# Odd units' half-precision casts on VectorE through all 192 units, in place of ScalarE from unit 37 on

## The chip, the cores and the metric

The kernel runs on one core of a Trainium2 chip. Its metric is the device time of one launch in microseconds (us), the median of several runs. The engines have their own in-order instruction streams and wait for each other through semaphores: PE (TensorE, matrix products; PEld is its weight load), DVE (VectorE), ACT (ScalarE), POOL (GpSimd) and SP (SyncE, which here issues the DMAs).

## The reference

Cluster attention is followed by a two-layer MLP. Each query and each key is assigned to the nearest of 16 centroids of its head; a query sees only keys of its own cluster.

```python
mask = q_assign[:, :, :, None] == k_assign[:, :, None, :]
scores = scale * np.matmul(q, k.transpose(0, 1, 3, 2))
scores = np.where(mask, scores, -1000000000.0)
scores = scores - np.max(scores, axis=-1, keepdims=True)
attn = np.exp(scores)
attn = attn / (np.sum(attn, axis=-1, keepdims=True) + 1e-09)
out = np.matmul(attn, v)              # 4 batches, 8 heads, 768 positions, 64 wide
# heads side by side: x is 3072 tokens by 512
h = x @ w_in                          # 512 to 2048
r = np.maximum(h, 0.0)
g = s * (r * r) + b
return g @ w_out                      # 2048 to 512
```

## The kernel before

Attention is cut into 192 units: one head and 128 queries against all 768 keys, in the order batch, chunk of 256 queries, pair of heads, row block, head. The MLP is cut into 192 steps: one chunk of 256 tokens and one block of 128 hidden columns. One loop with the counter i runs both: pass i issues unit i's scores and, 21 passes later (`LAG`), the MLP step that has become possible. So each pass after the beginning holds about one unit and one MLP step.

Single-precision accuracy comes from pairs of half-precision numbers: a value is cast to a high half, and the difference from the cast is the low half. For a unit this is done so:

- `scores`: PE makes the 128x768 scores in one of two PSUM buffers (`sc`, four products, L465).
- `maxima` and `exps`: DVE reduces the row maximum (L474); ACT makes the bias from it (L481) and then the exponentials `p` in single precision (L484). The score buffer is free after that, so PE can make the scores of unit i+2.
- `high`: the cast of `p` to half precision, the upper half of `ph` (L494, through the helper `copy`, whose ACT form has the line L120 and whose DVE and POOL forms have L122). This is the line of the change.
- `low`: POOL subtracts the cast from `p` for the lower half of `ph` (L516), and SP issues a DMA that transposes `ph` into `PT` (L518).
- `values`: PE multiplies `PT` with the two halves of v into the bank `px` (18 products a unit, L535 to L537), and DVE divides by the row sums (L543, L544, L547). `finish_x` splits the result into halves (ACT L558, POOL L561) and transposes it for the MLP (SP L564).

An MLP step is twelve products for `h` (L593) in a single PSUM bank, on ACT a relu that empties the bank (L600) and two squares (L602, L603), a subtraction on POOL for the low half `g` (L608), and six products into `acc` (L620). Beside this, one after the other, run the preparations of the next chunk's queries and the next batch's keys and values (`prep_q`, `prep_k`, `prep_v`): small chains that go through DVE (L102, L99, L69, L371, L188), PE (L98, L396), ACT (L186), POOL (L383, L293) and DMAs (`QA`, `QB`, `KA`, `KB`). The bank named `m` is shared by `px` and by these checks.

The first 16 units take another way (no cast, transposes on PE). Units 16 to 18 are cast on POOL. From unit 19, before the change, odd units up to 35 are cast on DVE, everything else on ACT; unit 37 is where the splitting of the weights, one block a pass for 16 passes, has ended. The order of instructions on each engine isn't that of the program's text: a scheduler places them with its own estimates of time, and so a change of engine in one place moves instructions on all engines.

Of the kernel before, what the change touches and what calls it, by code (L numbers as in the profile page):

```python
# [26 lines left out]
def tile_cluster_attention_mlp(ctx, tc, q, k, v, cent, w_in, w_out, s_in, b_in, out):  # L27
# [10 lines left out]
    NF = DFF // P  # L38
    HALF = S // 2
    V = nc.vector  # L40
    G = nc.gpsimd
    A = nc.scalar
    LAG = 21
# [74 lines left out]
    def copy(eng, dst, src):  # L118
        if eng is A:
            A.activation(dst, src, AF.Copy)  # L120
        else:
            eng.tensor_copy(dst, src)  # L122
# [366 lines left out]
    def high(i):  # L489
        u = U[i]  # L490
        if i < TURN:
            return
        u["ph"] = sb.tile([P, 2, S], F16, tag="big", name=f"ph_{i}", bufs=BIGN)
        copy(G if i < LAG - 2 else V if i < LAG + NF and i % 2 else A, u["ph"][:, 0, :], u["p"])  # L494

    def low(i):
        u = U[i]
# [220 lines left out]
    i = 0  # L718
    while i < NU + 8 or i - LAG < NS + 4:
# [10 lines left out]
        if 0 <= i - 1 < NU:  # L730
            with first_of_all(i):
                high(i - 1)
# [48 lines left out]
```

## Time and profile before

| | us |
|---|---|
| Median of 3 runs | 948.9 (946.03 to 953.5) |
| The profiled execution, its own time | 955.32 |
| Its span, first to last instruction | 953.6 |
| PE busy | 838.4 (88%) |
| ACT busy | 717.1 (75%) |
| DVE busy | 617.1 (65%) |
| POOL busy | 545.1 (57%) |

The profile has four parts in time. To about 140 us the first keys, queries and weights are prepared and PE waits often. From there to about 235 us the weights are split beside the first MLP steps. From 235 us (unit 37) to 882 us (the last cast) each pass holds a unit and an MLP step; this stretch is 647 us long. After 882 us the last MLP steps are left. A row of the profile gives line, engine, operation, tile written and tiles read, shapes, count, busy time, mean duration in ns and the idle time of the engine just before, with what ended it.

### The profile page before, as it was taken

The numbers are of one execution on the slowest core, as the hardware profiler recorded it, in microseconds if no ns is written. First come the engines' busy times: TensorE is split into PE (matmuls) and PEld (weight loads), VectorE is DVE, ScalarE is ACT, GpSimd is POOL, SyncE is SP. The second block draws the span as 40 slices with busy tenths as digits, with TensorE's granted clock in tenths as the row PEclk, the third lists the DMA queues.
The fourth block names the chain that finished last, engine by engine and source line by source line (L and its number), as shares of the span: only waits on it lengthen the run. The fifth ranks groups of instructions, "written<-read, shape, count | busy, mean of one in ns | idle before, by whom it ended". The sixth has DMA issues, their size and how long they took to land.

```text
span 953.6 us, 22551 instructions
## 1 busy us (share of the span) xinstructions
PE 838.4 (88%) x8673; PEld 587.2 (62%) x8673; DVE 617.1 (65%) x1416; ACT 717.1 (75%) x1406; POOL 545.1 (57%) x580
## 2 busy tenths in 40 slices
PE   0568565888999999999998999999999999999997
PEld 0456443565566666767666667666666767677664
DVE  7697888898577656657658667667766466463100
ACT  3476866877678878888777988977887888889443
POOL 3010115666566765777676767757867766676321
PEclk9966575999999999999999999999999999999999
DMA  6888813867777997887786898869779858786100
GB/s 171 217 220 242 238 34 77 200 143 123 178 134 144 200 192 136 167 175 144 144 171 139 196 187 162 165 139 200 131 156 181 149 119 158 137 161 141 33 23 23
DMA packets 437756, 144.23 MB, mean 151 GB/s; under 512 B 405392, under 2 KB 434064, under 8 KB 437648
## 3 DMA queue, kind: packets, MB, share of 16 engines
q1 hardware_dynamic: 437648, 142.78, 70.8%
q8 instruction: 68, 1.11, 0.5%
q14 instruction: 40, 0.33, 0.1%
HBM read 35.69 MB, written 6.29 MB: 44 GB/s over the span
## 4 chain that ended last, share of the span: by engine, by line
PE 31%; DVE 5%; DMA 5%; ACT 5%; POOL 4%; issue 4%; SPq 0%; POOLq 0%; DVEq 0%; ACTq 0%
PE h L593 12%; PE acc L620 11%; PE sc L465 4%; DMA qn<-in_q_dram 2%; POOL g L608 1%; POOL ph L516 1%; DMA kn<-in_k_dram 1%; PE px L535 1%; ACT p L484 1%; PE px L537 1%; PE px L536 1%; DVE ssm L474 1%; ACT ph L120 1%; DMA PT<-ph 1%; ACT r L600 1%
## 5 line engine op out<-in xcount | busy, mean ns | idle before, releaser
L516 POOL TENSOR_TENSOR ph<-p,ph 128x768 f16<-128x768 f32 x176 | 297.7, 1692 | 117.8 <-ACT ph L120 77.5
L620 PE MATMUL acc<-wos,g 128*128 128x512 f16 x1152 | 295.1, 380 | 3.6 <-POOL g L608 3.4
L593 PE MATMUL h<-x,wis 128*128 128x256 f16 x2304 | 288.1, 274 | 7.9 <-ACT r L600 3.7
L593 PEld LDWEIGHTS <-wis 128*128 128x128 f16 x2304 | 222.7, 98 | 59.4 <-issue 12.4
L474 DVE TENSOR_REDUCE ssm<-sc 128x1 f32<-128x768 f32 x192 | 181.8, 950 | 33.9 <-PE sc L465 33.3
L608 POOL TENSOR_TENSOR g<-r,g 128x256 f16<-128x256 f32 x192 | 133.3, 695 | 105.4 <-ACT r L603 103.0
L484 ACT ACTIVATE p<-sc,ssm,qsm 128x768 f32<-128x768 f32 x192 | 187.7, 978 | 1.5
L620 PEld LDWEIGHTS <-g 128*128 128x128 f16 x1152 | 104.4, 98 | 87.7 <-POOL g L608 7.2
L120 ACT ACTIVATE ph<-p 128x768 f16<-128x768 f32 x164 | 136.0, 830 | 5.2 <-DMA PT<-ph 2.9
L481 ACT ACTIVATE ssm<-ssm,lift,qsm 128x1 f32<-128x1 f32 x192 | 73.1, 381 | 87.1 <-DVE ssm L474 86.3
L600 ACT ACTIVATE r<-h,cf 128x256 f32<-128x256 f32 x192 | 89.2, 464 | 62.6 <-PE h L593 53.7
L535 PE MATMUL px<-vh,PT 128*128 128x65 f16 x1104 | 121.1, 196 | 9.0 <-DVE xs L547 2.4
L536 PE MATMUL px<-vl,PT 128*128 128x64 f16 x1104 | 121.0, 193 | 0.0
L537 PE MATMUL px<-vh,PT 128*128 128x65 f16 x1104 | 120.4, 195 | 0.7 <-DVE PT L514 0.7
L465 PE MATMUL sc<-KA,QA 128*128 128x384 f16 x384 | 100.1, 344 | 18.3 <-ACT p L484 15.4
L535 PEld LDWEIGHTS <-PT 128*128 128x128 f16 x1104 | 103.8, 98 | 19.3 <-issue 5.9
L536 PEld LDWEIGHTS <-PT 128*128 128x128 f16 x1104 | 103.6, 100 | 13.5 <-issue 4.8
L465 PE MATMUL sc<-KB,QB 128*128 128x384 f16 x384 | 100.6, 346 | 7.3 <-DMA QB<-qb 7.3
L537 PEld LDWEIGHTS <-PT 128*128 128x128 f16 x1104 | 103.7, 98 | 4.0 <-DVE PT L514 0.8
L602 ACT ACTIVATE g<-r 128x256 f16<-128x256 f32 x192 | 79.3, 413 | 4.3 <-PE acc L620 0.3
L603 ACT ACTIVATE r<-r 128x256 f32<-128x256 f32 x192 | 78.9, 411 | 3.5
L465 PEld LDWEIGHTS <-QA 128*128 128x128 f16 x384 | 36.0, 101 | 46.0 <-issue 20.4
(158 smaller groups left out, 1033.8 us busy)
## 6 DMA issues: line engine op xcount, KB each, us to landing
wst<-in_moe_w_in_dram SPq DMA_DIRECT2D x16, 512.0 KB, 4.5
wst<-in_moe_w_out_dram SPq DMA_DIRECT2D x16, 512.0 KB, 4.5
kn<-in_k_dram SPq DMA_DIRECT2D x16, 384.0 KB, 4.2
qn<-in_q_dram SPq DMA_DIRECT2D x24, 256.0 KB, 3.5
vn<-in_v_dram SPq DMA_DIRECT2D x16, 384.0 KB, 4.1
out_dram<-o SPq DMA_DIRECT2D x12, 512.0 KB, 3.5
PT<-ph SPq DMA_TRANSPOSE x176, 3.5
x<-xn SPq DMA_TRANSPOSE x48, 2.6
```

Of the source, the lines that this page charges most:

```text
L120: A.activation(dst, src, AF.Copy)
L465: last_score[0] = nc.tensor.matmul(sc[:, e, :HALF], X[:, col, :], y[:, h * S + e * HALF : h * S + (e + 1) * HALF], start=st, stop=not st)
L474: last_max[0] = V.tensor_reduce(SM[i // 4][:, 0, j : j + 1], U[i]["sc"], axis=AX.XY, op=ALU.max, negate=True)
L484: last_exp[0] = A.activation(p.rearrange("p (a b) -> p a b", a=2), u["sc"], AF.Exp, bias=bi, scale=u["scale"], **total)
L516: G.tensor_tensor(u["ph"][:, 1, :], u["p"], u["ph"][:, 0, :], op=ALU.subtract)
L535: nc.tensor.matmul(o1, PT[:, kt, :], vh[:, h, kt, : D + 1], start=(kt == 0), stop=False)
L536: nc.tensor.matmul(o, PT[:, kt, :], vl[:, h, kt, :], start=False, stop=False)
L537: nc.tensor.matmul(o1, PT[:, T + kt, :], vh[:, h, kt, : D + 1], start=False, stop=(kt == T - 1))
L593: nc.tensor.matmul(ph[:, :CW], WSP[ft][0][:, wl, kt, :], XS[(b, c, kt)][:, :, xl, :], start=(i == 0), stop=(i == len(terms) - 1))
L600: A.activation(r, ph[:, :CW], AF.Relu, scale=MS[(b, c)][0])
L608: G.tensor_tensor(g[:, 1, :], r, g[:, 0, :], op=ALU.subtract)
L620: nc.tensor.matmul(acc[:, t, :], g[:, gl, rows], WSP[ft][1][:, wl, :], start=(ft == 0 and gl + wl == 0), stop=(ft == NF - 1 and gl == 1))
```

## The change

Casts of odd units from 37 to 191 move from ACT to DVE. Even units stay on ACT. Nothing else is edited.

```diff
     def high(i):
         u = U[i]
         if i < TURN:
             return
         u["ph"] = sb.tile([P, 2, S], F16, tag="big", name=f"ph_{i}", bufs=BIGN)
-        copy(G if i < LAG - 2 else V if i < LAG + NF and i % 2 else A, u["ph"][:, 0, :], u["p"])
+        copy(G if i < LAG - 2 else V if i % 2 else A, u["ph"][:, 0, :], u["p"])
```

The scheduler moves other instructions too: 78 casts leave ACT and come to DVE, and from unit 37 on all five engines have rows in another order. Two places show it.

ACT at units 116 to 118, before. `p_117` is the exponential of unit 117, `ph_117` its cast, `r` and `g` are the MLP's relu and squares.

```order
L120 ACTIVATE ph_116_8871<-p_116_8805 128x768
L484 ACTIVATE p_117_8875<-sc_117_8860,ssm_116_8802,qsm_2_1_0_7950 128x768
L600 ACTIVATE r_2_0_0_8898<-h_2_0_0_8885,cf_2_0_8881 128x256
L602 ACTIVATE g_2_0_0_8900<-r_2_0_0_8898 128x256
L481 ACTIVATE ssm_116_8802<-ssm_116_8802,lift_132,qsm_2_1_0_7950 128x1
L603 ACTIVATE r_2_0_0_8898<-r_2_0_0_8898 128x256
L120 ACTIVATE ph_117_8999<-p_117_8875 128x768
L484 ACTIVATE p_118_9003<-sc_118_8984,ssm_116_8802,qsm_2_1_0_7950 128x768
```

The same place on ACT after the change.

```order
L120 ACTIVATE ph_116_8871<-p_116_8805 128x768
L484 ACTIVATE p_117_8875<-sc_117_8860,ssm_116_8802,qsm_2_1_0_7950 128x768
L481 ACTIVATE ssm_116_8802<-ssm_116_8802,lift_132,qsm_2_1_0_7950 128x1
L600 ACTIVATE r_2_0_0_8898<-h_2_0_0_8885,cf_2_0_8881 128x256
L602 ACTIVATE g_2_0_0_8900<-r_2_0_0_8898 128x256
L484 ACTIVATE p_118_9003<-sc_118_8984,ssm_116_8802,qsm_2_1_0_7950 128x768
```

The cast of the odd unit 117 no longer stands ahead of the exponential of unit 118; one of the squares has moved behind it as well.

DVE at units 175 and 176, before. The rows L543 to L547 are the division of a finished pair of units, `amb_q` a maximum in the preparation of queries.

```order
L474 TENSOR_REDUCE ssm_172_12886<-sc_175_13064 128x1
L543 TENSOR_SCALAR ssm_168_12622<-px_168_12977 128x2
L544 RECIPROCAL ssm_168_12622<-ssm_168_12622 128x2
L547 TENSOR_TENSOR xs_42_13016<-px_168_12977,ssm_168_12622 128x128
L102 TENSOR_REDUCE amb_q3_2_1_13144<-qn_3_2_1_13062 128x2
L543 TENSOR_SCALAR ssm_168_12622<-px_170_13103 128x2
L544 RECIPROCAL ssm_168_12622<-ssm_168_12622 128x2
L474 TENSOR_REDUCE ssm_176_13162<-sc_176_13149 128x1
```

The same place on DVE after the change.

```order
L474 TENSOR_REDUCE ssm_172_12886<-sc_175_13064 128x1
L102 TENSOR_REDUCE amb_q3_2_1_13144<-qn_3_2_1_13062 128x2
L122 CAST ph_175_13160<-p_175_13079 128x768
L543 TENSOR_SCALAR ssm_168_12622<-px_170_13103 128x2
L544 RECIPROCAL ssm_168_12622<-ssm_168_12622 128x2
L547 TENSOR_TENSOR xs_42_13016<-px_170_13103,ssm_168_12622 128x128
L474 TENSOR_REDUCE ssm_176_13162<-sc_176_13149 128x1
```

The cast of unit 175 stands between the maxima of units 175 and 176, ahead of a division that frees the shared bank. Of the 78 new casts 22 stand so, ahead of the next unit's maximum; 39 stand behind the maximum of unit i+1 and ahead of that of i+2, and 17 behind that one as well.

## The prediction

> **What bounds the kernel now.** First the page's busy times and clock, then busy times by stretch: before the change's first unit (35 us of it), the stretch in which it acts, and the end.
>
> ```profile
> PE 838.4 (88%) x8673; PEld 587.2 (62%) x8673; DVE 617.1 (65%) x1416; ACT 717.1 (75%) x1406; POOL 545.1 (57%) x580
> PEclk9966575999999999999999999999999999999999
> ...
> 200.00:235.00 35.00, 30.21 (x347) 20.80 (x348) 31.54 (x64) 27.17 (x56) 24.53 (x23) 1.00 0.70 140
> 235.00:882.00 647.00, 618.64 (x6815) 433.97 (x6813) 412.79 (x939) 524.96 (x1020) 448.01 (x447) 0.99 0.80 159
> 890.00:953.00 63.00, 57.89 (x434) 38.73 (x431) 6.15 (x20) 28.05 (x65) 15.39 (x23) 0.99 0.06 20
> ```
>
> The columns of the last three rows are stretch, length, then busy time of PE, PEld, DVE, ACT and POOL, clock, DMA share and GB/s. Units 37 to 191 lie in the middle row. There PE is busy 618.6 of 647.0 us (96%) at a clock of 0.99, so PE sets the pace and every other engine counts only as far as it makes PE wait. PE is without work for 28.4 us; that is about all that a better distribution can win by this view. ACT is next at 81%, then POOL at 69% and DVE at 64%. The last row has no cast in it: there the change can do nothing.
>
> Next, who made PE wait in the stretch (total us, times, longest):
>
> ```profile
> PE sc L465 <- ACT p L484: 4.3, 7, 1.1
> PE h L593 <- ACT r L600: 3.4, 6, 1.3
> PE pq L396 <- DMA QA<-qa: 3.3, 4, 1.1
> PE am_q L98 <- DVE ksm L99: 3.1, 2, 1.9
> PE h L593 <- DMA x<-xn: 2.7, 3, 1.4
> PE sc L465 <- DMA QB<-qb: 1.9, 2, 1.5
> PE px L535 <- DVE qsm L99: 1.8, 2, 1.5
> PE am_q L98 <- DVE xs L547: 1.7, 2, 1.4
> PE acc L620 <- POOL g L608: 1.6, 3, 0.7
> PE px L535 <- DVE xs L547: 1.4, 1, 1.4
> PE am_q L98 <- DVE amb_q L102: 0.8, 1, 0.8
> PE px L535 <- DVE oe_k L288: 0.7, 1, 0.7
> PE am_q L98 <- DVE vm L99: 0.4, 1, 0.4
> PE pq L396 <- DVE xs L547: 0.3, 1, 0.3
> ```
>
> By releaser: ACT 4.3 + 3.4 = 7.7 us; DVE 3.1 + 1.8 + 1.7 + 1.4 + 0.8 + 0.7 + 0.4 + 0.3 = 10.2 us; DMAs 3.3 + 2.7 + 1.9 = 7.9 us; POOL 1.6 us. ACT is the busier engine, but PE waits more for DVE, mostly in the short checks that share one PSUM bank.
>
> **The change part by part.** What the casts cost on each engine, and what else runs there in the stretch (from the groups by line, and from the rows of the tile `ph`, which give min/median/max in ns):
>
> ```profile
> L516 POOL TENSOR_TENSOR ph<-p,ph x176: 1632/1644/2356, 138.2 to 881.7; 128x768 f16<-128x768 f32 x176
> L120 ACT ACTIVATE ph<-p x164: 825/827/845, 161.9 to 880.8; 128x768 f16<-128x768 f32 x164
> L122 DVE CAST ph<-p x9: 531/551/1017, 159.8 to 235.6; 128x768 f16<-128x768 f32 x9
> ...
> L122 DVE CAST ph<-p 128x768 f16<-128x768 f32 x9 | 5.8, 647 | 0.0
> L120 ACT ACTIVATE ph<-p 128x768 f16<-128x768 f32 x164 | 136.0, 830 | 5.2 <-DMA PT<-ph 2.9 <-DMA KA<-ka 2.0
> L474 DVE TENSOR_REDUCE ssm<-sc 128x1 f32<-128x768 f32 x155 | 146.8, 950 | 26.6 <-PE sc L465 26.0
> ```
>
> *What leaves ACT.* The odd numbers from 37 to 191 are 78, and 78 x 0.830 = 64.7 us leave ACT: 525.0 falls to 460.3, 81% to 71%. In the order before, each of these casts stands directly ahead of the next exponential, as at unit 118, so that exponential can come up to 0.83 us sooner and its score buffer is free sooner. A wait behind a queue grows with its busy time over its free time; I scale with that ratio as an estimate. For ACT it is 525.0/122.0 = 4.3 before and 460.3/186.7 = 2.5 after, a factor 0.57, and 0.43 x 7.7 = **3.3 us less**. The ends are nothing (some of these waits start earlier, at a maximum on DVE) and all 7.7.
>
> *What comes to DVE.* The same cast exists there nine times, at 0.647 us in the mean: 78 x 0.647 = 50.5 us, so DVE goes from 412.8 to 463.3 (72%). The nine come from a time when POOL was no busier (24.5 of 35 us, 70%, against 69%), but one took 1.017 where the least is 0.531, so the price depends on POOL, as these rows of single instructions, and the two groups on DVE that also read two tiles in SBUF, show:
>
> ```profile
> 567.94 1.49 DVE L371 TENSOR_TENSOR qsm<-qsm,ksm 128x2 f32<-128x2 f32 x1
> 567.74 1.67 POOL L516 TENSOR_TENSOR ph<-p,ph 128x768 f16<-128x768 f32 x1 [0.79 <-ACT ph L120]
> L371 DVE TENSOR_TENSOR qsm<-qsm,ksm x24: 141/161/1493, 15.9 to 833.1; 128x2 f32<-128x2 f32 x24
> ...
> L188 DVE SCALAR_TENSOR_TENSOR ka<-kn,ksm,ka x10: 1007/1606/2394, 265.3 to 701.3; 128x768 f16<-128x768 f32 x10
> ...
> L188 DVE SCALAR_TENSOR_TENSOR ka<-kn,ksm,ka 128x768 f16<-128x768 f32 x10 | 16.3, 1628 | 4.1 <-ACT ka L186 4.1
> ```
>
> An operation on two numbers a lane took 1.49 us instead of 0.16 and ended when POOL's subtraction did; the subtraction beside it, which had begun first, took its normal time. The larger `ka` operation loses 1628 - 1007 = 621 ns in the mean. If casts fared as badly they would take 0.531 + 0.621 = 1.152 us, 89.9 us in all. I take the 0.647, the row of the cast itself.
>
> The Trainium skill (SBUF — State Buffer, section "Who interferes with whom") speaks against the change here: a VectorE copy or cast in a two-port mode and a GpSimd instruction shut each other out of a shared port pair, and the one that comes second waits for the whole instruction of the first. The trace agrees for L371 (1.49 us against 0.16); by this rule a cast that comes just after the start of a subtraction would take some 0.55 + 1.64 = 2.2 us (an estimate with the trace's durations), which no cast of this trace shows.
>
> How much of this reaches PE? The cast also adds a wait: DVE has to hold at it until ACT has made `p`. Behind it in DVE's queue stand the next maximum (for which ACT's bias L481 and then the exponential wait) and the division that frees the bank (for which PE waits). For 56 of the 78 the next maximum behind the cast is of unit i+2 or later, whose scores need the buffer that this same exponential frees; there the cast runs while PE refills the buffer and its cover is 0.65 us of PE work. For 22, as at unit 175, it is not so. With the ratio as for ACT: 412.8/234.2 = 1.76 becomes 463.3/183.7 = 2.52, a factor 1.43, and 0.43 x 10.2 = **4.4 us more**. The ends are nothing (all covered) and, at 89.9 us, 502.7/144.3 = 3.48, a factor 1.98, 10.0 us.
>
> *What POOL and the DMAs do.* POOL's subtraction of an odd unit, with its transpose on SP's queue, can start 0.83 - 0.55 = 0.28 us sooner; `PT` is read four passes later, so this wins nothing. Against it, a cast on DVE shuts POOL out as in the rows above, in the other direction (L516's longest is 2.356 against 1.644). If casts meet POOL as often as it is busy (69%), it loses 0.69 x 78 x 0.531 = 28.6 us: 448.0/199.0 = 2.25 becomes 476.6/170.4 = 2.80, a factor 1.24. POOL's own wait and the three DMAs that end chains through it make 1.6 + 7.9 = 9.5 us, and 0.24 x 9.5 = **2.3 us more**; the ends are 2 us less (their ACT links, L186 and L558, come sooner) and, were every cast to meet POOL (78 x 0.531 = 41.4 us), 3.6 us more.
>
> *The rest.* The clock of PE is full and stays so: nothing, within 3 us either way (the mean of 0.99 leaves 0.01 x 647 = 6 us, of which I let half come or go). The first 235 us and the MLP's end keep their instructions: nothing.
>
> The sum is -3.3 + 4.4 + 2.3 = +3.4 us. The profiled execution took 955.3 us, its span of 953.6 and 1.7 around it, and would take 958.7. It is 6.4 us above the median of 948.9, and the difference carries over to the median: 948.9 + 3.4, so **952 us**. The ends of the terms give -7.7 + 0 - 2 - 3 = -12.7 and 0 + 10.0 + 3.6 + 3 = +16.6, that is 936 to 966.
>
> **The rivals.** *ACT was what counted (faster).* If all waits for ACT go (7.7) and with them those for work that starts from ACT, the subtraction `g` (1.6, after L603) and `x` (2.7, after L558), while DVE's 234 us of free time swallows the casts, the time is 948.9 - 12.0 = 936.9. For it speak these waits of the other engines in the stretch:
>
> ```profile
> POOL ph L516 <- ACT ph L120: 77.5, 66, 2.8
> ACT ssm L481 <- DVE ssm L474: 69.2, 67, 3.4
> POOL g L608 <- ACT r L603: 50.5, 47, 2.9
> ```
>
> POOL waits for ACT 128 us in these rows. Against it speaks the middle one: ACT itself waits 69.2 us for DVE's maxima, so what leaves ACT is partly bought with a later maximum.
>
> *DVE's queue is held at the cast (slower).* The place is the 22 casts that stand ahead of the next unit's maximum. There the maximum waits for the exponential and for the cast. If POOL runs as it does beside `ka`, each costs 1.15 us, 22 x 1.15 = 25.3, and with 3.3 back from ACT the time is 948.9 + 22.0 = 970.9; at the casts' own 0.647 it is 14.2 - 3.3, 959.8. The middle is 965. It decides where PE has less than a cast's length to spare at that point. The rule of the skill named above is this rival's reason for the longer casts. Against it: only 26.0 us of DVE's idle time in the row of L474 ends with PE, so DVE often has the scores waiting and isn't on the path each time.
>
> *The new order (either way, rather slower).* The scheduler has moved rows on every engine. If half of some 28 preparations in the stretch (18 of queries, 10 of keys by the group counts) gain a wait like those for `QA` (3.3/4 = 0.8 us), that is 14 x 0.8 = 11.2 us: 960.
>
> ```profile
> L383 POOL COPY qa<-qb 128x512 f16<-128x512 f16 x18 | 13.7, 760 | 0.0
> L333 POOL COPY kb<-ka 128x768 f16<-128x768 f16 x10 | 8.3, 834 | 12.7 <-ACT ka L186 12.4
> ```
>
> That the change does not do what it says is excluded by the order: 78 more casts on DVE, as many less on ACT.
>
> **How the numbers follow.** 1% is 9.5 us (939.4 to 958.4), about what a measurement can tell from no change. My sum has a chance of 0.55: 0.45 within 1%, and 0.10 above by its upper end. ACT's relief has 0.17, counted as faster. The held queue has 0.20, counted as slower. The new order has 0.08: 0.05 slower, 0.03 within. So faster 0.17, same 0.48, slower 0.35. The range is 936 (the lower end, which nearly holds the first rival) to 970 (which nearly holds the second).
>
> **What would show it.** Right: in the stretch ACT near 460 us busy and DVE near 463; a DVE cast of 0.6 to 0.7 us in the mean; PE's waits for `p` and `r` down by some 3 us and those for `ksm`, `qsm` and `xs` up by more. Wrong: casts of 1 us or more with L474's rows later (held queue); PE's waits for DVE unchanged and the stretch over 9 us shorter (ACT's relief); DVE's waits unchanged but `QA`, `QB` or `x` waits doubled (order). A change in the first 235 us or after the last cast would make the whole working wrong.

## The result, and the profile after

The changed kernel takes 964.75 us (median of 4 runs, 961.98 to 968.27) against 951.2 us for the kernel before (4 runs, 946.03 to 956.42): a ratio of 1.012, 95% interval 1.0082 to 1.0157 (the two medians alone would give 1.014; ratios are given as recorded, with their intervals). It is slower by a little more than the 1% that the prediction set as the bound of what can be told.

The profiled execution took 965.98 us, its span is 964.3. First the busy times of the page and the groups that the change touches; the columns are as before.

```profile
PE 836.0 (87%) x8673; PEld 585.6 (61%) x8673; DVE 662.3 (69%) x1494; ACT 667.6 (69%) x1328; POOL 547.5 (57%) x580
...
L120 ACT ACTIVATE ph<-p 128x768 f16<-128x768 f32 x86 | 71.4, 830 | 3.7 <-POOL ph L516 3.2
L122 DVE CAST ph<-p 128x768 f16<-128x768 f32 x87 | 55.7, 640 | 14.9 <-ACT p L484 6.3
```

The change does what it says: 78 casts fewer on ACT, 78 more on DVE, and a cast on DVE takes 640 ns in the mean, where 647 was taken for the sum. DVE and ACT are now equally busy, at 69%. ACT's casts fell by 64.6 us (136.0 to 71.4), but its busy time by only 49.5 (717.1 to 667.6): neighbouring rows on ACT overlap, as where an exponential starts at 342.80, takes 0.99 us and the next row starts at 343.69, and busy time counts an overlap once. PE has no less work than before and needs longer for it.

Where the time went shows when the two executions are cut at the same two places, the start of the exponential of unit 37 and the end of the last exponential. Before:

```profile
0.00:239.00 239.00, 157.64 (x1380) 111.37 (x1381) 200.08 (x461) 162.35 (x317) 81.10 (x110) 0.81 0.68 167
239.00:880.60 641.60, 613.47 (x6774) 430.68 (x6774) 409.82 (x933) 521.53 (x1014) 444.40 (x442) 0.99 0.80 159
880.60:953.60 73.00, 67.29 (x522) 45.16 (x519) 7.19 (x24) 33.27 (x77) 19.59 (x28) 0.99 0.11 30
```

After:

```profile
0.00:241.00 241.00, 153.75 (x1380) 109.23 (x1381) 200.83 (x462) 162.57 (x317) 81.29 (x110) 0.84 0.67 165
241.00:896.10 655.10, 619.85 (x6790) 434.09 (x6790) 453.01 (x1009) 474.58 (x942) 447.05 (x444) 0.99 0.77 156
896.10:964.20 68.10, 62.44 (x505) 42.26 (x502) 8.45 (x25) 30.42 (x71) 19.15 (x27) 0.98 0.13 32
```

The stretch grew by 13.5 us and the end shrank by 4.9, because PE did more of the MLP within the stretch (6.4 us more busy time there, 4.9 less in the end). What is left is 13.5 - 4.9 = 8.6 us. Of it 7.1 us are idle time of PE (33.8 us in stretch and end before, 40.9 after) and 1.5 us a longer busy time for the same products. Another 2.0 us lie ahead of unit 37 (241.0 against 239.0). They are not the change's: in the two traces the rows of every engine are the same up to 242 us, so this is a difference between two executions of the same rows, and not the change in the first part that the prediction had named as a sign against it. The waits of PE in the stretch say where its idle time went:

```profile
PE acc L620 <- POOL g L608: 5.8, 8, 1.4
PE h L593 <- ACT r L600: 5.0, 8, 1.3
PE pk L346 <- DVE xs L547: 3.9, 2, 2.3
PE pq L396 <- DMA QA<-qa: 3.3, 2, 1.7
PE sc L465 <- ACT p L484: 3.2, 4, 1.7
PE am_q L98 <- DVE xs L547: 2.4, 2, 1.7
PE h L593 <- DMA x<-xn: 2.3, 3, 1.5
PE sc L465 <- DMA QB<-qb: 2.2, 1, 2.2
PE px L535 <- DVE xs L547: 1.6, 2, 1.4
PE px L535 <- DVE cf L582: 1.3, 1, 1.3
PE px L535 <- DVE xm L584: 1.0, 1, 1.0
PE px L535 <- DVE xm L99: 0.9, 1, 0.9
PE pq L396 <- DVE xs L547: 0.8, 2, 0.6
PE am_q L98 <- DVE amb_q L102: 0.6, 1, 0.6
PE px L535 <- DVE qsm L65: 0.6, 1, 0.6
PE px L535 <- DVE qsm L99: 0.3, 1, 0.3
```

| PE waits in the stretch for | before | after |
|---|---|---|
| ACT | 7.7 | 8.2 |
| DVE | 10.2 | 13.4 |
| DMAs | 7.9 | 7.8 |
| POOL | 1.6 | 5.8 |
| sum | 27.4 | 35.2 |

The sum rose by 7.8 us, about the 7.1 of idle time. ACT gave nothing back although its busy time in the stretch is 47 us less. Of what came on top, 4.2 us are POOL's, all at `g`, and 3.2 DVE's. This is one execution of each kernel, and runs of the kernel before alone spread from 946.03 to 956.42 us, so a difference of a few us in one row is a sign and no proof. How it comes about can be read at one place. The rows are those of DVE, POOL and PE near 347 us, around the cast of unit 59, whose `p` was ready at 343.79.

```profile
346.45 0.95 DVE L102 TENSOR_REDUCE vm<-vn 128x1 f32<-128x768 f32 x1 [3.24 <-DMA vn<-in_v_dram]
347.32 0.55 DVE L122 CAST ph<-p 128x768 f16<-128x768 f32 x1
...
347.95 1.64 POOL L516 TENSOR_TENSOR ph<-p,ph 128x768 f16<-128x768 f32 x1 [4.11 <-DVE ssm L543]
349.55 0.67 POOL L608 TENSOR_TENSOR g<-r,g 128x256 f16<-128x256 f32 x1
...
350.28 0.39 PE L620 MATMUL acc<-wos,g 128*128 128x512 f16 x1 [1.24 <-POOL g L608]
```

DVE stood 3.24 us at a step of the preparation of v whose load had not landed; the cast stood behind it, though its input was there. POOL, in order too, stood 4.11 us at that unit's subtraction (the profile names L543, the row behind the cast; the cast itself had ended at 347.87), and the MLP's `g`, whose inputs had been ready since 346.1, stood behind the subtraction. PE waited 1.24 us for it. Six of the eight waits for `g`, 4.9 of the 5.8 us, look like this: the subtraction last or last but one ahead of `g` on POOL had stood 1.3 to 4.1 us for a cast on DVE, and in five of the six DVE had just stood 0.5 to 3.7 us at a load of the preparations. So an engine with 31% free time was waited for, because one late instruction held its queue.

### The profile page after: what moved, and what is told of

It is laid out like the page before. It is cut to its first block, busy times and chain, and to the rows that moved or that the text cites. A ratio compares the mean times of both kernels' runs of the same rounds, so it can differ in the third digit from the quotient of the medians.

```text
span 964.3 us, 22610 instructions
## 1 busy us (share of the span) xinstructions
PE 836.0 (87%) x8673; PEld 585.6 (61%) x8673; DVE 662.3 (69%) x1494; ACT 667.6 (69%) x1328; POOL 547.5 (57%) x580
## 4 chain that ended last, share of the span: by engine, by line
PE 37%; DVE 11%; DMA 5%; issue 4%; POOL 3%; ACT 3%; SPq 1%; POOLq 0%; DVEq 0%; ACTq 0%
PE h L593 13%; PE acc L620 13%; PE sc L465 5%; DVE ssm L474 3%; DMA qn<-in_q_dram 2%; PE px L535 1%; POOL ph L516 1%; PE px L537 1%; PE px L536 1%; DMA kn<-in_k_dram 1%; DVE ph L122 1%; POOL g L608 1%; DMA PT<-ph 1%; DVE ka L188 1%; DVE qa L188 1%
## 5 line engine op out<-in xcount | busy, mean ns | idle before, releaser
L620 PE MATMUL acc<-wos,g 128*128 128x512 f16 x1152 | 298.4, 382 | 7.6 <-POOL g L608 7.4
L120 ACT ACTIVATE ph<-p 128x768 f16<-128x768 f32 x86 | 71.4, 830 | 3.7 <-POOL ph L516 3.2
L122 DVE CAST ph<-p 128x768 f16<-128x768 f32 x87 | 55.7, 640 | 14.9 <-ACT p L484 6.3
```

Of the source, the lines that this page charges most:

```text
L620: nc.tensor.matmul(acc[:, t, :], g[:, gl, rows], WSP[ft][1][:, wl, :], start=(ft == 0 and gl + wl == 0), stop=(ft == NF - 1 and gl == 1))
```

## The experiments

Each time stands against runs of the kernel before taken beside it on the same chip: 953.9 us for the scratch tile, the relief, the even units and the quarter, 956.9 for tiny, late, and the two with early loads, 957.2 for the rest. Every edit below also leads the scheduler to another order; only the two halves of the pair with the order held fixed share one.

**What DVE's work costs alone.** 78 extra casts on DVE into a tile that nobody reads:

```diff
+        if i >= LAG + NF and i % 2:
+            V.tensor_copy(sb.tile([P, 640], F16, tag="dup", name=f"dup_{i}", bufs=1), u["p"][:, :640])
```

> The kernel before, with 78 extra casts on VectorE for the odd units from 37 on (640 of the 768 columns, into a scratch tile that nobody reads); ScalarE keeps its casts, nothing waits for the new ones. It prices VectorE's added work without a dependence on it. Theory (GpSimd's subtraction waits in order for a cast that is late in VectorE's queue, and the MLP's subtraction and TensorE wait behind it): only VectorE's share of the loss appears, 2 to 5 us over the kernel before (TensorE's waits for VectorE up by about 3 us, its wait for GpSimd's g unchanged at 1.6 us). Rival (VectorE's load alone, through its queue and its port): at least the whole loss, 12 us or more, since nothing is taken from ScalarE. Rival (the new order alone): anything, with no tie to these waits.

975.28 us, ratio 1.0224 (1.0198 to 1.0251): 21 us slower. The group of these casts in the stretch, and the row of their tile with min/median/max:

```profile
L496 DVE CAST dup<-p 128x640 f16<-128x640 f32 x78 | 67.9, 871 | 26.4 <-ACT p L484 26.2
...
L496 DVE CAST dup<-p x78: 477/832/1960, 240.6 to 898.2; 128x640 f16<-128x640 f32 x78
```

These casts are smaller than the real ones and take longer: 871 ns in the mean, 477 at the least, against 640 and 535 for the 768 columns of the changed kernel. Here ACT makes the unit's own cast, so POOL can subtract while DVE casts. The timeline shows what that costs: 59 of the 78 began while a POOL instruction ran; they took 995 ns in the mean, and 58 of them ended after it. The others took 477 to 495. In the changed kernel POOL's subtraction of the same unit waits for the cast and cannot run beside it, but other POOL instructions do: 31 of its 87 casts began beside one and took 798 ns in the mean, the other 56 took 535 to 561. PE's waits for DVE rose from 10.2 to 19.3 us, those for `g` from 1.6 to 3.7. The loss agrees with the rival that spoke of load and port, and not with my theory of late casts, which would have left 2 to 5 us.

**What ACT's relief is worth alone.** The second square of the MLP is left out from the second chunk on, so the low half of `g` is not computed from the right number:

```diff
-        A.activation(r, r, AF.Square)
+        if b + c == 0:
+            A.activation(r, r, AF.Square)
```

> The kernel before without ScalarE's second square (the single-precision square of r, 0.41 us) in all MLP steps but those of the first chunk, so the low half of g is computed from r and the output is not the reference's; it takes about 63 us from ScalarE in the stretch, as much as the change does, and puts nothing on VectorE. It prices ScalarE's relief, from above, because it also shortens the path to g. Theory of the prediction (relief is worth 3.3 us, at most 7.7): 941 to 948 with the kernel before at about 951. Rival (TensorE does not wait for ScalarE's work at all, only for what is ahead of it): within 2 us of the kernel before.

958.0 us, ratio 1.0039 (1.0015 to 1.0064). The row of the stretch from 235 to 882 us, to be set beside 524.96 us of ACT before:

```profile
235.00:882.00 647.00, 615.27 (x6730) 432.57 (x6728) 415.28 (x935) 469.81 (x857) 444.74 (x445) 0.99 0.81 157
```

55 us are gone from ACT, and the kernel is no faster, rather 0.4% slower. Neither expectation holds: the time did not fall, and it is 4.1 us over the kernel before, beyond the rival's 2. An engine's work was taken away, with no work added anywhere, and PE's waits for ACT were 9.3 us in the stretch against 7.7. The scheduler had moved rows here as well, which is the likely reason; this run does not separate it.

**Other units.** The even units on DVE in place of the odd ones, and a quarter of the units:

```diff
-  V if i % 2 else A
+  V if (i % 2 if i < LAG + NF else i % 2 == 0) else A     # even
+  V if (i % 2 if i < LAG + NF else i % 4 == 1) else A     # quarter
```

> From unit 37 on the even units are cast on VectorE and the odd ones on ScalarE; 77 casts in place of 78. Theory (late casts in VectorE's queue hold GpSimd): as slow as the change, 8 to 16 us over the kernel before, with the wait of TensorE for g again at 4 us or more. Rival (the new order alone): the loss depends on which units they are, so it can be anything from none to twice as much.

> From unit 37 on only every fourth unit (i % 4 == 1, 39 of the 78) is cast on VectorE. Theory: each cast adds its part, so about half of the loss, 4 to 8 us over the kernel before. Rival (a balance: some relief of ScalarE wins before VectorE's queue loses): faster than the kernel before by 2 to 6 us. Rival (the new order): no relation to the half.

Even: 957.91 us, ratio 1.0054 (1.0034 to 1.0074). Quarter: 958.61 us, ratio 1.0055 (1.0031 to 1.0078). The same load on DVE costs about half as much when it is the other units', and half the load costs as much as that. The quarter fits the theory's half, but the even units do not fit any price per cast: they are 4.0 us over the kernel before, where the theory said 8 to 16, and PE's waits for `g`, put at 4 us or more, are 1.3.

**The wait at the head of the queue.** The extra casts again, but of 2 columns, so that they hold the queue until `p` is there and do little work; then the same from a constant, so that they do not wait either:

```diff
+            V.tensor_copy(sb.tile([P, 2], F16, tag="dup", name=f"dup_{i}", bufs=1), u["p"][:, :2])   # tiny
+            V.tensor_copy(sb.tile([P, 2], F16, tag="dup", name=f"dup_{i}", bufs=1), rev[:, :2])      # tiny, no wait
```

> The kernel before with 78 extra casts on VectorE as in the run with the scratch tile, but of 2 columns in place of 640, so they add almost no work; each still holds VectorE's queue until ScalarE has made p, and 32 of them stand ahead of the next unit's maximum. Theory (the wait at the head of VectorE's queue is what costs): half or more of that run's loss of some 21 us stays, 10 us or more over the kernel before. Rival (the work itself, and the port it shares with GpSimd): within 4 us of the kernel before.

> The kernel before with 78 extra casts of 2 columns on VectorE at the odd units' places, as in the tiny run, but from a constant, so that none waits for ScalarE's p. Theory (the wait at the head of VectorE's queue cost the tiny run its 8 us): within 3 us of the kernel before. Rival (any other order costs, since the scheduler re-places everything): 5 us or more over the kernel before, though nothing waits and nothing is added.

Tiny: 965.23 us, ratio 1.0101 (1.0054 to 1.0148), 8.4 us over the kernel before and so between the two expectations. Tiny without a wait: 966.17 us, ratio 1.0084 (1.0056 to 1.0112), 8.9 us over it, by the number on the rival's side. The two can't be told apart, but the second run is no control for the first. A copy of a constant is ready from the start, and the scheduler put it there; the row of the tile with min/median/max and the first and last start, then the time to the exponential of unit 37 and from there to the end:

```profile
L496 DVE CAST dup<-rev x78: 158/167/815, 1.0 to 47.6; 128x2 f16<-128x2 f32 x78
...
0.00:248.30 248.30, 158.43 (x1415) 112.64 (x1416) 208.99 (x548) 162.95 (x318) 84.46 (x110) 0.80 0.65 161
248.30:967.70 719.40, 679.90 (x7260) 473.73 (x7258) 418.26 (x947) 555.87 (x1090) 467.40 (x470) 1.00 0.73 145
```

All 78 copies ran in the first 48 us and none at the odd units' places. The kernel reaches unit 37 at 248.3 us, 9.3 later than the kernel before (239.0), and takes 719.4 us from there, 4.8 longer than its 714.6 (each in its profiled execution). So about two thirds of the loss arose before any of the places in question, and this run does not show that the loss is there when nothing waits. The tiny run stays without a control: its 1.0% can be the wait, the new order or the work, for beside POOL even these casts took long, 0.52 us in the mean where the least is 0.155.

**The cast later in the program.** In the changed kernel, the odd unit's `high` is called behind the next unit's maximum and exponential:

```diff
-        if 0 <= i - 1 < NU:
+        cast_late = i - 1 >= LAG + NF and i % 2 == 0
+        if 0 <= i - 1 < NU and not cast_late:
             with first_of_all(i):
                 high(i - 1)
...
                 exps(i)
+        if 0 <= i - 1 < NU and cast_late:
+            high(i - 1)
```

> The changed kernel with the odd units' casts placed behind the next unit's maximum and exponential in the program; on VectorE 1 of the 78 then stands ahead of the next unit's maximum, where it was 22, and 51 ahead of the one after. Theory (the maximum held behind the cast costs): at most a third of the loss stays, 4 us or less over the kernel before. Rival (VectorE's added work as such, or GpSimd held by late casts): as slow as the change or slower, 10 us or more over the kernel before, since the casts come later still.

966.37 us, ratio 1.01 (1.0056 to 1.0145). One held maximum in place of 22, and the loss is that of the change within the intervals, 9.5 us over the kernel before. The 22 casts ahead of the next maximum are then hardly what cost, though this kernel has an order of its own. PE's waits for `g` are still 4.3 us.

**Earlier loads, as a pair.** The loads of the queries are issued one pass earlier, in the changed kernel and in the kernel before:

```diff
         )
         yield
+        if b + c:
+            yield
...
-                    at(s0, prep_q(b, c, hq))
+                    at(s0 - 1, prep_q(b, c, hq))
```

> The changed kernel with the queries' loads issued one pass earlier and the preparation otherwise at its old place, so that VectorE does not stand at a maximum over queries that are not there yet, with casts behind it. Theory (casts late behind a preparation step that waits for a DMA): the loss against the same edit of the kernel before falls by a third or more, to 8 us or less. Rival (VectorE's waits for these loads cost nothing): the loss stays at 11 us or more.

> The kernel before with the queries' loads issued one pass earlier, as the other half of the pair. Theory: VectorE's 51 us of waits for these loads fall to 15 or less, and the time falls by 2 to 6 us. Rival (these waits are covered): within 2 us of the kernel before.

Changed: 956.53 us, ratio 1.0002 (0.9978 to 1.0025). Before: 952.79 us, ratio 0.9957 (0.9933 to 0.9982). The loss of the change is 956.53/952.79, 0.4%, in place of 1.2%. That agrees with the theory's number, but not cleanly with its reason: DVE's waits for the queries' loads fell only from 31.8 to 21.8 us in the changed kernel and from 51.1 to 34.9 in the kernel before, not to 15. Nor did the hold through POOL go: PE waits 5.9 us for `g` in the changed kernel and 0.5 in the other, while its waits for DVE are 4.6 us against 14.4.

**The order held fixed.** With the scheduler's estimates of time off, PE has the same 8673 products and as many weight loads in the same order with and without the change. Apart from the casts themselves no row moves on DVE, 4 on ACT, 16 on POOL and 3 on SP; in the change as it was measured at least 179, 194, 90 and 33 rows moved on these engines (rows outside the longest common sequence of the two traces), and PE's order changed too.

```diff
-    with _tile.TileContext(nc, schedule_with_timeline_sim=True) as tc:
+    with _tile.TileContext(nc, schedule_with_timeline_sim=False) as tc:
```

> The kernel before with the scheduler's estimates of time turned off, so that another, fixed order results; it is one half of a pair in which TensorE's order is the same row for row with and without the change. By itself: slower than the kernel before by some per cent in any theory; only the pair counts.

> The changed kernel in the same way. Theory (the place of the cast itself costs: VectorE's queue holds it, GpSimd and TensorE wait behind): 7 us or more over the other half of the pair. Rival (the new order was the loss, the cast on VectorE by itself costs little): within 4 us of the other half, or faster by ScalarE's relief.

Without the change 989.41 us (5 runs, ratio to the kernel before 1.033, 1.0301 to 1.0358), with it 988.17 us (6 runs, 1.0316, 1.0287 to 1.0345). The change costs nothing here that could be told: -0.1%, with intervals that overlap almost whole; that is what the rival had said. PE's waits in this pair, from 236 to 905 us, first without the change:

```profile
PE h L593 <- ACT r L600: 23.4, 20, 3.2
PE pk L346 <- DVE xs L547: 12.8, 5, 6.5
PE h L593 <- DMA x<-xn: 5.7, 5, 2.2
PE px L535 <- DVE oe_q L288: 3.0, 3, 1.5
PE am_q L98 <- DVE xs L547: 2.2, 2, 1.1
PE acc L620 <- DVE o L628: 1.8, 5, 0.4
```

With the change:

```profile
PE pk L346 <- DVE xs L547: 15.4, 4, 7.0
PE acc L620 <- POOL g L608: 13.7, 8, 3.1
PE h L593 <- ACT r L600: 9.5, 13, 2.8
PE h L593 <- DMA x<-xn: 2.5, 1, 2.5
PE pq L396 <- DVE xs L547: 2.4, 1, 2.4
PE am_q L98 <- DVE xs L547: 1.9, 2, 1.1
```

POOL's waits at the subtraction with the change; without it they are 155.4 us for ACT's casts and nothing for DVE:

```profile
POOL ph L516 <- ACT ph L120: 77.3, 66, 2.2
POOL ph L516 <- DVE ssm L543: 52.3, 33, 5.3
POOL ph L516 <- DVE ph L122: 48.7, 34, 5.0
```

Here both of the change's effects stand clear of each other. PE's waits for ACT fall from 23.4 to 9.5 us: the relief exists. Its waits for `g` rise from nothing to 13.7 us: the hold through POOL exists too, at subtractions that wait 101.0 us for a cast on DVE (L543 is the row behind it). In these two executions the two are of one size, 13.9 and 13.7. The executions shown took 991.70 and 984.64 us, 7 us apart where the medians are 1.2 apart, so the balance is no closer than that. DVE's part hardly moves (19.8 and 19.7), although in this order all 78 casts stand ahead of the next unit's maximum. So a maximum held behind a cast costs PE nothing here.

**Another order of the same work.** Within a pass, the running preparations are advanced in the reverse sequence; every instruction stays on its engine:

```diff
-        for gen in list(active):
+        for gen in list(active)[::-1]:
```

> The kernel before with the running preparations advanced in the reverse sequence within each pass; no instruction is added, removed or given to another engine, but all engines' orders differ. Theory (waits at the cast): no reason for a loss, within 4 us of the kernel before. Rival (any other order costs): 4 to 12 us over the kernel before.

946.82 us, ratio 0.9886 (0.9859 to 0.9913): faster than the kernel before by 1.1%. The stretch and the end of its profiled execution, cut at the same two places as above:

```profile
236.70:877.00 640.30, 616.44 (x6790) 432.64 (x6786) 419.92 (x928) 523.41 (x1020) 450.31 (x446) 1.00 0.79 160
877.00:944.70 67.70, 62.00 (x503) 42.02 (x499) 7.22 (x24) 30.83 (x72) 18.50 (x27) 0.98 0.14 32
```

It reaches unit 37 2.3 us sooner, and stretch and end together take 708.0 us against 714.6, with the engines as busy as before: PE stood idle 23.9 us in the stretch, against 28.1. It is the fastest version of this study and beats both kernels. I had not expected that, and neither the theory nor the rival said it: no order was to gain.

## Why the prediction was right or wrong

The time of 964.75 us lies in the range of 936 to 970, and slower was the side of the forecast; but 952 was forecast, a loss within 1%, and the most likely case did not come. The loss is three to four times the sum's +3.4 us, and the upper part of the range, in which the time lies, was made for another mechanism, the held maxima. To that extent the range held by luck. By the prediction's steps:

- *PE bounds the kernel, and only its waits count.* Right: PE's busy time is the same within 2.4 us, and the rise of its waits (7.8 us) is about that of its idle time (7.1) and most of what stretch and end grew by (8.6).
- *What the cast costs on DVE.* Right: 640 ns against 647 taken. The upper end, 1.15 us from the `ka` row, is what a single cast can take when it begins beside a POOL instruction (the longest took 1.227), but only 31 of 87 did. The 2.2 us estimated for a cast that comes just after the start of a subtraction came for none of these; the longest extra cast of 640 columns took 1.960.
- *What leaves ACT and comes to DVE.* Mis-sized as busy time: in the stretch ACT stands at 474.6 us, not 460.3, and DVE at 453.0, not 463.3, mainly since busy time counts overlapping rows once.
- *ACT's relief, -3.3 us.* Measured +0.5. In the scheduled kernel it did not come. The fixed order shows that it can: -13.9 us, from waits for ACT that are three times as long. The step took each cast to stand directly ahead of the next exponential; in the trace before, 41 of the 78 do. The scaling by busy time over free time failed here, since it supposes that the queue in front of an engine is all that changes.
- *DVE's part, +4.4 us.* Measured +3.2, the right size, but not as described. Its reason with the 22 held maxima has little left: with one held maximum the loss was still 1.0%, and in the fixed order all 78 are held and PE's waits for DVE do not grow. Of the waits named as signs, those for `ksm` went and those for `xs` rose from 3.4 to 8.7 us.
- *POOL and the DMAs, +2.3 us.* Measured +4.1, all of it at `g` (1.6 to 5.8) and nothing at the DMAs. The step named the wrong way: POOL was to lose 28.6 us to the port, and its busy time rose by 2.4 (545.1 to 547.5). What cost was POOL's order, in which `g` stands behind a subtraction that waits for a cast that waits in DVE's queue. The prediction looked at what stands behind the cast on DVE; what stood ahead of it, and who stood behind its reader on POOL, mattered more.
- *The new order.* It was given a chance of 0.08, by waits for `QA` that did not grow (3.3 us before and after). That order matters is shown: the same work in another order won 1.1% (reversed), and 55 us less work on ACT in another order cost 0.4% (relief). A loss of 1% by order alone is not shown: the run that was to show it put its copies into the first 48 us. With the order fixed, the change costs nothing.

What is settled: the cast's own price; that PE waits longer for `g` with the change in all three pairs of traces (1.6 to 5.8 us as measured, 0.5 to 5.9 with early loads, 0 to 13.7 with the order fixed), as measured and with the order fixed behind subtractions that wait for a cast on DVE; and that the scheduler's re-placing of rows alone can move this kernel by 1.1%. What goes with the order is the rest: PE's waits for ACT changed by +0.5 us as measured and by -13.9 with the order fixed, those for DVE by +3.2, -9.8 with early loads and -0.1 with the order fixed. What stays open: how the 1.2% divides between the hold, the work on DVE beside POOL, and the order. They could not be separated in the scheduled kernel, since every edit of it gave another order. The fixed order is 3% slower and has longer waits for ACT to win back, so its zero need not hold in the exact order of the kernel before; that order with only the casts moved was not tried.

## What to carry to other kernels

Where a scheduler places instructions by its own estimates, an edit that moves work between engines is two changes: the work, and a new order everywhere. Before a loss or gain of a per cent is put down to the work, time a version that changes the order and no work, and the pair with the order fixed. Then look in the trace where the rows of such a control ran: copies that wait for nothing were moved to the start of the program and controlled for nothing. When work moves to an engine that is less busy, read not only its free time but what stands ahead in its queue and waits for a load, and what stands behind the moved step's reader.

## What was not expected of the hardware

Two casts of nearly the same size took 640 ns (768 columns, followed by POOL's subtraction) and 871 ns (640 columns, beside it) in the mean, at least 535 and 477 ns. The exclusion between VectorE and GpSimd that the Trainium skill describes (SBUF — State Buffer, section "Who interferes with whom") shows in both. In the changed kernel a cast that did not begin beside a POOL instruction took 535 to 561 ns. Of the 31 that did, the 22 that met more than 0.2 us of it all ended 0.41 to 0.42 us after that instruction did, so that the longest took 1.227 us. The difference between the two kernels is how many casts meet POOL, 31 of 87 against 59 of 78: a dependence keeps the subtraction of the same unit away from its cast, but not POOL's other work.
